# Tanh over two PSUM banks in the last group but one, and newly written instruction orders, in a fused linear-attention and tanh-shrink kernel

## The chip, the cores and the metric

The kernel runs on one core of one Trainium2 chip. The time is device microseconds (us) of one execution. Before the change three runs gave 104.94, 103.58 and 104.55 us, a median of 104.55. Engines are named as the profile names them: PE (TensorE matmuls), PEld (its weight loads), DVE (VectorE), ACT (ScalarE), POOL (GpSimd), SP (SyncE, which here only issues DMAs). PSUM, the memory that PE writes, has 8 banks here, each 512 float32 columns on 128 partitions.

## The reference

Batch 4, heads 4, sequence 1088, head size 32, sketch size 8, feed-forward width 2048.

```python
def phi(x):                        # 32 -> 64 features, a product of two sketches
    a = einsum('rd,bhsd->bhsr', S1, x)
    b = einsum('rd,bhsd->bhsr', S2, x)
    return einsum('bhsi,bhsj->bhsij', a, b).reshape(..., 64)
q_p, k_p = phi(q), phi(k)
kv  = einsum('bhsf,bhsd->bhfd', k_p, v);   z = sum(k_p, axis=2)
num = einsum('bhsf,bhfd->bhsd', q_p, kv)
den = einsum('bhsf,bhf->bhs', q_p, z)[..., None] + 1e-6
x   = (num / den) laid out as 4352 tokens x 128
h   = x @ w_in                     # 128 -> 2048
out = (h - tanh(h)) @ w_out        # 2048 -> 128
```

## The kernel before

The work has two halves. The **attention front** makes `xT` (128 features x 4352 tokens, bf16) in five chunks, called u=0 to u=4: batch 0 in two chunks, the other three batches in one each. The **layers** take the tokens in nine groups, g=0 to g=8: eight of 512 columns and a last one of 256. A group needs the chunks that hold its tokens: groups 0 and 1 need chunks 0 and 1, group 2 needs chunk 2, group 4 needs chunk 3, and groups 6, 7 and 8 need chunk 4.

In a group there are 16 blocks of 128 hidden units. For each, `h<n>` (L809) is one matmul of `w_in` by `xT` into a PSUM bank, `t<n>` (L813, or L818) is the tanh on ACT from that bank into the SBUF tile `tt`, and `o<n>` (L867, or L832 in the last group) is one matmul of `w_out` by the tanh that adds into PSUM bank 7. n counts through: h0 to h15 are group 0, h16 to h31 are group 1, and so on to h128 to h143, which are group 8. The part of the output that is linear, h times w_out, doesn't go through the hidden layer: `wp` multiplies the two weights once, split in a high and a low bf16 part (`whi`, `wlo`), and `lin<g>.whi` and `lin<g>.wlo` (L859; L832 for group 8) are two matmuls a group into the same bank 7. In all groups but group 0 they come first and clear the bank. After the last o of a group, `out<g>` (L872) on DVE transposes bank 7 into `osb`, which four or eight DMAs on SP store (`st<g>...`). So `lin` of the next group has to wait for `out` of the group before, since there is one accumulator, and all the o of the group stand behind their `lin`. Group 8 has its own accumulators, banks 0 and 1.

An h of a single tanh takes bank 4, 5 or 6 by n mod 3. A group in the list `PAIRS` puts two h side by side and has one tanh for both: before, this is group 8 alone, where two h of 256 columns share one bank.

The names in the front that matter below, with b the batch and u the chunk: `k<b>`, `q<b>`, `v<b>` are loads; `kT` a transpose on DVE (L511); `kp` a projection on PE (L522); `kab` its transpose on DVE (L528); `wk` products on DVE and POOL (L543); `sum` the matmuls of the key products with v (L591); `gram` and `fold` (L554, L578) the denominators; `qp` a projection on PE (L696); `qab`, `au`, `dn`, `rd`, `an`, `qm`, `qt` steps on DVE (`qm` half on POOL) that end in transposed query products; `num` (L741) the matmuls into banks 0 to 3; `x<u>` (L764) the copy to `xT`. `wi0` to `wi3` and `wo0`, `wo1` are loads of the two weights, `wic` and `woc` the casts to bf16 (`wic1` and both `woc` on POOL).

What stands where is not found by a scheduler at run time. `ORDERS` holds one list of names for each engine, and the instructions are emitted in that order; `SESSIONS` is a list of names that says in which order the users of a PSUM bank follow each other; `GATES` adds waits (a<b: a waits for b). `P.arranged` reads the three, and `sync` then places semaphore waits where one engine needs another's result. Each engine runs its list in order, so that a waiting instruction holds all that stand behind it. An entry such as `*12` in the list of PE is twelve matmuls on zeros ahead of the real work.

Of the kernel before, what the change touches and what calls it, by code (L numbers as in the profile page):

```python
# [971 lines left out]
```

## Time and profile before

| | |
|---|---|
| three runs | 104.94, 103.58, 104.55 us |
| the profiled execution | 103.87 us, of which the span of the profile is 102.1 us |
| busy: PE, ACT, DVE, PEld, POOL | 95.2, 79.2, 63.3, 44.0, 22.8 us |
| DMA | 11.74 MB, 115 GB/s over the span |
| matmuls h (L809) and o (L867) | 144 and 128, 45.8 and 39.5 us busy |
| tanh of 512 columns (L813) | 128, 66.8 us busy, 603 ns each |
| first and last tanh | start at 15.52 and 97.98 us |

Busy time of PE counts each matmul from its start to its modelled end, and the next one starts before that, so that the distance between two starts says more than the length of one. All times within the execution are counted from the start of the span.

### The profile page before, as it was taken

Reading aid. Unit: us, or ns where it says so; the run is one execution under the profiler, and the core shown is the slowest. Engines: PE = TensorE matmul, PEld = TensorE weight load, DVE = VectorE, ACT = ScalarE, POOL = GpSimd, SP = SyncE. Lnnn points to the kernel's source line nnn. Section 1 sums busy time; section 2 is a strip of 40 time slices with the busy share of each in tenths; the row PEclk is TensorE's granted clock in tenths of the full one; section 3 lists DMA queues with packets and bytes.
Section 4 is the critical chain, followed back from the end, with each engine's and each line's share of the span. In section 5 each row is a group of like instructions: output and inputs, shape, how many; then the busy total and the mean of one; then the engine's idle time right before and its main releaser. Section 6 shows DMA issues by size and latency. Waiting matters only on the chain.

```text
span 102.1 us, 2878 instructions
## 1 busy us (share of the span) xinstructions
PE 95.2 (93%) x1215; PEld 44.0 (43%) x1215; DVE 63.3 (62%) x109; ACT 79.2 (78%) x158; POOL 22.8 (22%) x36
## 2 busy tenths in 40 slices
PE   5978977989999999999999999999999999999980
PEld 2314632334736654334653334344334444435660
DVE  4589887999699998999968629595080020020210
ACT  4105428998889282599999999999999999998770
POOL 5306243085463160054080000700000000000000
PEclk9999999999999999999999999999999999999999
DMA  2899999997997059009700110035003204204143
GB/s 59 253 270 293 350 344 281 271 258 66 230 231 220 20 65 285 9 0 155 217 7 6 29 26 0 6 55 89 8 0 53 43 6 85 50 9 72 22 77 80
DMA packets 26012, 11.74 MB, mean 115 GB/s; under 512 B 19984, under 2 KB 24208, under 8 KB 26000
## 3 DMA queue, kind: packets, MB, share of 16 engines
q1 hardware_dynamic: 25712, 11.42, 49.4%
q8 instruction: 9, 0.15, 0.6%
q10 hardware_dynamic: 288, 0.15, 0.5%
q14 instruction: 3, 0.02, 0.1%
HBM read 8.81 MB, written 2.23 MB: 108 GB/s over the span
## 4 chain that ended last, share of the span: by engine, by line
PE 69%; DVE 12%; DMA 9%; SPq 5%; issue 1%
PE ps L809 26%; PE ps L867 25%; DMA kraw<-in_k_dram 9%; PE ps L741 5%; PE ps L859 4%; PE ps L591 2%; PE ps L696 2%; PE ps L832 2%; DVE qab L702 2%; DVE qp L719 2%; SPq L473 2%; DVE qpT L726 2%; DVE kT L511 1%; PE ps L522 1%; SPq L458 1%
## 5 line engine op out<-in xcount | busy, mean ns | idle before, releaser
L813 ACT ACTIVATE tt<-ps 128x512 bf16<-128x512 f32 x128 | 66.8, 603 | 6.1 <-PE ps L809 5.1
L809 PE MATMUL ps<-xT,w_in 128*128 128x512 bf16 (+1 forms) x144 | 45.8, 369 | 0.9 <-ACT tt L813 0.6
L867 PE MATMUL ps<-tt,w_out 128*128 128x512 bf16 x128 | 39.5, 379 | 0.1
L809 PEld LDWEIGHTS ps<-xT,w_in 128*128 128x128 bf16 x144 | 13.3, 98 | 20.9 <-ACT tt L813 9.0
L872 DVE STREAM_TRANSPOSE osb<-ps 128x512 f32<-128x512 f32 x8 | 5.7, 715 | 20.3 <-PE ps L867 20.3
L867 PEld LDWEIGHTS ps<-tt,w_out 128*128 128x128 bf16 x128 | 12.4, 98 | 13.4 <-issue 0.9
L719 POOL TENSOR_TENSOR qp<-an,qab 128x1152 f32<-128x1152 f32 (+1 forms) x4 | 7.8, 1953 | 21.6 <-DVE an L713 11.2
L543 POOL TENSOR_TENSOR wk<-kab 128x384 f32<-128x384 f32 (+2 forms) x8 | 9.0, 1126 | 13.7 <-DVE wk L543 13.2
L726 DVE STREAM_TRANSPOSE qpT<-qp 128x1152 f32<-128x1152 f32 (+1 forms) x8 | 9.8, 1229 | 1.1 <-POOL qp L719 1.0
L764 DVE CAST xT<-ps 128x576 bf16<-128x576 f32 (+2 forms) x7 | 4.4, 681 | 5.1 <-PE ps L741 5.1
L543 DVE TENSOR_TENSOR wk<-kab 128x768 f32<-128x768 f32 (+2 forms) x7 | 5.8, 842 | 0.9 <-PE ps L591 0.8
L511 DVE STREAM_TRANSPOSE kT<-kraw 128x512 f32<-128x512 f32 (+1 forms) x8 | 5.5, 718 | 1.2 <-DMA kraw<-in_k_dram 1.2
L702 DVE STREAM_TRANSPOSE qab<-ps 128x1152 f32<-128x1152 f32 (+1 forms) x4 | 5.0, 1239 | 1.9 <-PE ps L696 1.8
L741 PE MATMUL ps<-qpT,ndw 32*32 32x288 f32 (+3 forms) x256 | 5.7, 373 | 0.2 <-DVE qpT L726 0.2
L623 DVE STREAM_TRANSPOSE qT<-qraw 128x1088 f32<-128x1088 f32 (+2 forms) x5 | 5.3, 1070 | 0.0
L409 PE MATMUL ps<-wz 128*128 128x512 bf16 x12 | 4.2, 524 | 1.2 <-DVE wz L416 1.2
L719 DVE TENSOR_TENSOR qp<-an,qab 128x1152 f32<-128x1152 f32 (+1 forms) x4 | 5.1, 1276 | 0.1
L818 ACT ACTIVATE tt<-ps 128x512 bf16<-128x512 f32 x8 | 4.3, 598 | 0.8 <-PE ps L809 0.7
L591 PE MATMUL ps<-wk,vx 128*32 128x64 f32 x288 | 4.9, 220 | 0.1
L591 PEld LDWEIGHTS ps<-wk,vx 128*32 128x32 f32 x288 | 4.2, 110 | 0.9 <-issue 0.6
L741 PEld LDWEIGHTS ps<-qpT,ndw 32*32 32x32 f32 x256 | 2.5, 103 | 2.9 <-issue 1.2
L522 PE MATMUL ps<-kT,wkm 64*32 64x288 f32 x64 | 2.9, 415 | 0.7 <-DVE kT L511 0.7
(90 smaller groups left out, 73.7 us busy)
## 6 DMA issues: line engine op xcount, KB each, us to landing
kraw<-in_k_dram SPq DMA_DIRECT2D x3, 544.0 KB, 9.7
qraw<-in_q_dram SPq DMA_DIRECT2D x3, 544.0 KB, 4.7
out_dram<-osb SPq DMA_DIRECT2D x20, 64.0 KB, 1.9
vx<-in_v_dram SPq DMA_DIRECT2D x8, 144.0 KB, 4.3
vx<-in_v_dram SPq DMA_DIRECT2D x8, 128.0 KB, 4.2
w_in_f<-in_moe_w_in_dram SPq DMA_DIRECT2D x4, 256.0 KB, 9.4
w_out_f<-in_moe_w_out_dram SPq DMA_DIRECT2D x2, 512.0 KB, 10.0
kraw<-in_k_dram SPq DMA_DIRECT2D x1, 288.0 KB, 3.3
```

The source lines that it names most:

```text
L511: P.op(f"kT{b}.{cs[0]}", "vector", dve(hi - lo), lambda e, cs=cs, n=n, lo=lo, hi=hi: e.transpose(out=kT[i][:, 0:n, cs[0]:cs[1] + 1, :].rea ...
L543: P.op(f"wk{b}.{n0}", eng, (dve if eng == "vector" else pool)(64 * n), lambda e, n0=n0, n1=n1, n=n, a_=a_: e.tensor_tensor(out=wk[0][:, n0 ...
L591: ins = e.matmul(ps[32 * h:32 * h + 32, SB, 0:64], vx[i][:, h, t, :], wk[0][:, 4 * t + h, :], start=(t == 0), stop=(t == 8), tile_position ...
L623: P.op(f"qT{b}.{lo}", "vector", dve(32 * (hi - lo)), lambda e: e.transpose(out=dst, in_=src), r=[("qraw", i, c) for c in range(lo, hi)], w ...
L702: P.op(f"qab{u}", "vector", dve(32 * n), lambda e: e.transpose(out=qab[ui][:, 0:n, :].rearrange("p (h t) x -> p h t x", h=H), in_=ps[:, b0 ...
L719: P.op(f"qm{u}.{h0}", eng, (pool if eng == "gpsimd" else dve)(64 * (n1 - n0)), lambda e, n0=n0, n1=n1, b_=b_: e.tensor_tensor(out=qp[ui][: ...
L726: P.op(f"qt{u}.{h0}", "vector", dve(64 * (n1 - n0)), lambda e, n0=n0, n1=n1: e.transpose(out=qpT[ui][:, n0:n1, :, :].rearrange("p n y j -> ...
L741: ins = e.matmul(ps[32 * h:32 * h + 32, ct, 0:32 * own[ct]], ndw[i][32 * ct:32 * ct + 32, y, 32 * h:32 * h + 32], qpT[ui][32 * ct:32 * ct ...
L809: P.op(f"h{s}", "tensor", pe(n), lambda e, jb=jb, bk=bk, col=col: e.matmul(ps[:, bk, col:col + n], w_in[:, 128 * jb:128 * jb + 128], xT[:, ...
L813: P.op(f"t{s}", "scalar", act(n), lambda e, ts=ts, bk=bk: e.activation(out=tt[:, ts, 0:n], in_=ps[:, bk, 0:n], func=AF.Tanh, scale=-1.0), ...
L867: P.op(f"o{slot + jb}", "tensor", pe(n), lambda e, jb=jb, ts=ts: e.matmul(acc[:, 0:n], w_out[:, jb, :], tt[:, ts, 0:n], start=late and jb ...
L872: P.op(f"out{g}", "vector", dve(n), lambda e: e.transpose(out=osb[u][:, 0:n], in_=acc[:, 0:n]), r=ka, w=[("osb", u)], prio=when)
```

## The change

Three things change together. First, group 7 joins `PAIRS`: its 16 tanh of 512 columns become 8 of 1024, each over two neighbouring banks. The two banks of a pair were written as 2, 3 and 0, 1 in turn for such a group; now they are 2, 3 and 4, 5. Second, all five lists of `ORDERS`, `SESSIONS` and four of the `GATES` are written anew. Third, two settings are added that do nothing at the values given: `ENDS` is empty, so the last store is the one of before, and `K1CUTS` has one piece, so the load of `k1` is the one of before.

```diff
-PAIRS = (8,)
+PAIRS = (7, 8)
+ENDS = ()
+K1CUTS = ((0, 1088),)
...
-*12 kp0 qB0 gram0 qA0 zs eps1 fold0 eps0 sum0.0 den0 den1 kwt num0.1 num0.0 turn0 h0 qp1 h2 h1 h3 o0 h4 o1 h5 h6 kp1
+*13 kp0 qB0 gram0 qA0 fold0 eps1 zs eps0 sum0.0 den0 den1 kwt num0.0 num0.1 turn0 h0 h1 qp1 h2 o0 h3 h4 o1 o2 h5 h6
...
-k0.1 s1 k0.0 q0.0 v0.0 v0.1 v0.2 v0.3 q0.1 wi0 wo0 k1.0 wi1 wi2 wi3 v1.1 v1.2 k2.0 wo1 v1.3 v1.0 q1.0 wT v2.0 v2.2
+k0.1 s1 k0.0 q0.0 v0.0 v0.1 v0.2 v0.3 wi0 q0.1 k1.0 wo0 wi1 wi2 wi3 v1.3 v1.0 k2.0 v1.1 v1.2 wo1 q1.0 wT v2.3 v2.0
...
-identb<wk2.0 wic1<wk0.0 woc0<wk0.0 woc1<wk1.24 wk0.22<wk0.0 wk0.29<wk0.0 qm1.2<qm1.0 wk1.12<qm1.0 wk1.30<qm1.0
-qm2.2<qm2.0 wk2.12<wk2.24 wk2.30<wk2.0 qm3.2<qm3.0 wk3.12<wk3.24 wk3.30<wk3.24 qm4.2<an4
+identb<qm2.0 wic1<wk0.0 woc0<wk0.0 woc1<wk1.0 wk0.22<wk0.0 wk0.29<wk0.0 qm1.2<qm1.0 wk1.12<qm1.0 wk1.30<qm1.0
+qm2.2<qm2.0 wk2.12<wk2.24 wk2.30<wk2.0 qm3.2<qm3.0 wk3.12<qm2.0 wk3.30<qm2.0 qm4.2<qm4.0
...
             if g in PAIRS:
                 x, bk, col = s // 2, 4 + s // 2 % 3, 256 * (jb % 2)
                 if n > 256:
-                    bk, col = (2, 0)[s // 2 % 2] + jb % 2, 0
+                    bk, col = (2, 4)[s // 2 % 2] + jb % 2, 0
                 kh = bank(f"h{s - jb % 2}", bk)
...
-    load_k(1, 0, S, L + 11)
+    for x, (lo, hi) in enumerate(K1CUTS):
+        load_k(1, lo, hi, L + 11 + 0.1 * x, x)
```

Line numbers of the changed kernel are 2 higher from the settings on, and 8 or 9 higher behind the store of the last group: h is L811, the tanh of a pair L820, o L875, `lin` L867.

What the new lists move is seen best in the built programs, at three places: the start of the layers (SP and PE), the last groups (PE and ACT), and the loads of `v3` (SP). At the start, the loads on SP from the second piece of `q0` on, before the change:

```order
L464 DMA qraw<-in_q_dram 128x576
L479 DMA w_in_f<-in_moe_w_in_dram 128x512
L483 DMA w_out_f<-in_moe_w_out_dram 128x8x128
L458 DMA kraw<-in_k_dram 128x1088
L479 DMA w_in_f<-in_moe_w_in_dram 128x512 x3
```

The same place after the change:

```order
L481 DMA w_in_f<-in_moe_w_in_dram 128x512
L466 DMA qraw<-in_q_dram 128x576
L460 DMA kraw<-in_k_dram 128x1088
L485 DMA w_out_f<-in_moe_w_out_dram 128x8x128
L481 DMA w_in_f<-in_moe_w_in_dram 128x512 x3
```

The first quarter of `w_in` now goes ahead of the rest of `q0`, and `k1` goes ahead of the first half of `w_out`.

On PE the first matmuls of the layers, from `turn0` (ident by kvz) to the sixth or seventh h (xT by w_in), with `qp1` (qT by wq) and the first o (tt by w_out) between, before the change:

```order
L610 MATMUL ps<-ident,kvz 128x128 x2
L809 MATMUL ps<-xT,w_in 128x512
L696 MATMUL ps<-qT,wq 32x160 x16
L809 MATMUL ps<-xT,w_in 128x512 x3
L867 MATMUL ps<-tt,w_out 128x512
L809 MATMUL ps<-xT,w_in 128x512
L867 MATMUL ps<-tt,w_out 128x512
L809 MATMUL ps<-xT,w_in 128x512 x2
```

The same place after the change:

```order
L612 MATMUL ps<-ident,kvz 128x128 x2
L811 MATMUL ps<-xT,w_in 128x512 x2
L698 MATMUL ps<-qT,wq 32x160 x16
L811 MATMUL ps<-xT,w_in 128x512
L875 MATMUL ps<-tt,w_out 128x512
L811 MATMUL ps<-xT,w_in 128x512 x2
L875 MATMUL ps<-tt,w_out 128x512 x2
L811 MATMUL ps<-xT,w_in 128x512 x2
```

The first o stood behind four h and stands behind three; h3 and h4, which were ahead of and behind it, are both behind it now.

In the last groups, on PE, the passage from group 5 to group 6, from the last five or so o (tt by w_out) of group 5 to `lin6` (xT by whi and by wlo), before the change:

```order
L867 MATMUL ps<-tt,w_out 128x512 x3
L809 MATMUL ps<-xT,w_in 128x512
L867 MATMUL ps<-tt,w_out 128x512
L809 MATMUL ps<-xT,w_in 128x512
L867 MATMUL ps<-tt,w_out 128x512
L832 MATMUL ps<-wlo,xT 128x128 x2
L809 MATMUL ps<-xT,w_in 128x512 x3
L859 MATMUL ps<-xT,whi 128x512
L859 MATMUL ps<-xT,wlo 128x512
```

The same place after the change:

```order
L811 MATMUL ps<-xT,w_in 128x512 x2
L875 MATMUL ps<-tt,w_out 128x512 x5
L811 MATMUL ps<-xT,w_in 128x512 x5
L867 MATMUL ps<-xT,whi 128x512
L867 MATMUL ps<-xT,wlo 128x512
```

Between the last o of group 5 and `lin6` there were three h (and the small `lin8.wlo`, which moves to near the end); now there are five h, two of which are h116 and h117 of group 7.

On ACT, the tanh from `ndw3` (a copy of the last batch's sums) on, before the change:

```order
L616 COPY ndw<-ps 128x256
L813 ACTIVATE tt<-ps 128x512 x73
L818 ACTIVATE tt<-ps 128x2x256 x8
L846 COPY osr<-ps 128x128
```

The same place after the change:

```order
L618 COPY ndw<-ps 128x256
L815 ACTIVATE tt<-ps 128x512 x47
L820 ACTIVATE tt<-ps 128x1024
L815 ACTIVATE tt<-ps 128x512 x9
L820 ACTIVATE tt<-ps 128x1024
L815 ACTIVATE tt<-ps 128x512
L820 ACTIVATE tt<-ps 128x1024 x2
L820 ACTIVATE tt<-ps 128x2x256
L820 ACTIVATE tt<-ps 128x1024 x4
L820 ACTIVATE tt<-ps 128x2x256 x7
L848 COPY osr<-ps 128x128
```

The tanh of groups 6, 7 and 8 are mixed: the first pair of group 7 (t112) stands among the single tanh of group 6, ahead of its last nine but one, and the first pair of group 8 (t130) among those of group 7.

At the third place, on SP, from the load of `k3` or its neighbours to the first stores, with the loads of `v3` (vx) between, before the change:

```order
L458 DMA kraw<-in_k_dram 128x1088
L879 DMA out_dram<-osb 32x16x32
L464 DMA qraw<-in_q_dram 128x1088
L473 DMA vx<-in_v_dram 32x4x288
L879 DMA out_dram<-osb 32x16x32 x3
L473 DMA vx<-in_v_dram 32x4x256
```

The same place after the change:

```order
L466 DMA qraw<-in_q_dram 128x1088
L460 DMA kraw<-in_k_dram 128x1088
L466 DMA qraw<-in_q_dram 128x1088
L887 DMA out_dram<-osb 32x16x32
L475 DMA vx<-in_v_dram 32x4x288
L887 DMA out_dram<-osb 32x16x32
L475 DMA vx<-in_v_dram 32x4x256
L475 DMA vx<-in_v_dram 32x4x288
```

`q2` and `q3` now go ahead of all stores. Of the four loads of `v3`, two stood behind the first store and three do now. That first store was `st0.0.0`, of group 0; now it is `st1.0.2`, of group 1, which waits for `out1`. Before, the first store of group 1 stood three stores later, with one load of `v3` behind it.

88 lines of the change are left out of this document (47 added, 41 removed).

## The prediction

> **What bounds the kernel.** I began with the page: busy times, the chain that ended last, and the costliest groups.
>
> ```profile
> span 102.1 us, 2878 instructions
> PE 95.2 (93%) x1215; PEld 44.0 (43%) x1215; DVE 63.3 (62%) x109; ACT 79.2 (78%) x158; POOL 22.8 (22%) x36
> PE 69%; DVE 12%; DMA 9%; SPq 5%; issue 1%
> L813 ACT ACTIVATE tt<-ps 128x512 bf16<-128x512 f32 x128 | 66.8, 603 | 6.1 <-PE ps L809 5.1
> ```
>
> The chain is on PE for 69% of the span, and ACT, whose work the change makes less, waits for PE (5.1 us at L813) and holds little of the chain. So the question is not what the wider tanh saves, but how long PE stands. I cut the time into stretches, of which two late ones are these (columns: PE, PEld, DVE, ACT, POOL busy, each with its instructions, then granted clock, DMA share, GB/s).
>
> ```profile
> 82.00:90.00 8.00, 8.00 (x39) 3.49 (x38) 0.72 (x1) 7.68 (x16) 0.00 (x0) 1.00 0.26 45
> 90.00:98.00 8.00, 7.94 (x59) 4.64 (x58) 1.44 (x2) 6.77 (x14) 0.00 (x0) 1.00 0.20 33
> ```
>
> PE is all but full in both. But its ends are modelled and overlap the next start, so short stands don't show in a busy share. They show in the distance of starts, in the timeline of PE:
>
> ```profile
> 36.93 1.67 PE L867 MATMUL ps<-tt,w_out 128*128 128x512 bf16 x7
> ...
> 65.25 1.03 PE L809 MATMUL ps<-xT,w_in 128*128 128x512 bf16 x3
> 66.30 0.39 PE L859 MATMUL ps<-xT,whi 128*128 128x512 bf16 x1
> ...
> 75.88 0.38 PE L809 MATMUL ps<-xT,w_in 128*128 128x512 bf16 x1
> 76.28 0.39 PE L859 MATMUL ps<-xT,whi 128*128 128x512 bf16 x1
> ...
> 82.88 0.97 PE L809 MATMUL ps<-xT,w_in 128*128 128x512 bf16 x3
> 83.82 0.39 PE L859 MATMUL ps<-xT,whi 128*128 128x512 bf16 x1
> ...
> 89.87 1.02 PE L809 MATMUL ps<-xT,w_in 128*128 128x512 bf16 x3
> 90.92 0.39 PE L859 MATMUL ps<-xT,whi 128*128 128x512 bf16 x1
> ```
>
> Seven o take 1.67 us, the last of them some 0.38, so one follows the other after (1.67 - 0.38) / 6 = 0.215 us. Three h should thus take 0.65 us until the next start. Ahead of lin4 they took 1.05 (a stand of 0.40), ahead of lin6 0.94 (0.29), ahead of lin7 1.05 (0.40), and the one h ahead of lin5 took 0.40 (0.18). Together **1.27 us of standing at the four passages between groups**. What ends them is the accumulator:
>
> ```profile
> 65.03 0.38 PE L867 MATMUL ps<-tt,w_out 128*128 128x512 bf16 x1
> 65.52 0.72 DVE L872 STREAM_TRANSPOSE osb<-ps 128x512 f32<-128x512 f32 x1 [1.25 <-PE ps L867]
> ```
>
> From the start of the last o (65.03) to lin4 (66.30) lie 1.27 us: the o, the transpose of 0.72 us, two hand-overs. In that time only h are free to run, and only as far as their banks are.
>
> **The change part by part.** *Wide tanh.* What one of 1024 columns takes, no row shows. Nearest rows of ACT:
>
> ```profile
> 50.72 0.37 ACT L604 COPY kvz<-ps 128x256 f32<-128x256 f32 x1
> 96.53 2.07 ACT L818 ACTIVATE tt<-ps 128x512 bf16<-128x512 f32 x4 [0.21 <-PE ps L809]
> ```
>
> One alone takes 0.60 us (603 ns above); four follow each other after (2.07 - 0.60) / 3 = 0.49. From 256 to 512 columns a row grows by 0.60 - 0.37 = 0.23 us, so 1024 columns hold ACT for between 2 x 0.46 = 0.92 us (growth alone) and two whole rows, 1.20; I take 0.95, near the growth, since the rows overlap. Against 0.98 for two this saves 8 x 0.03 = 0.2 us of ACT, or costs 1.8 at the other end. ACT has 1.2 us free between 90 and 98 (6.77 of 8.00), so I count the saving at nothing, and at the bad end 1.8 - 1.2 = 0.6 us.
>
> *Banks.* This is what I expect the gain from. Group 7 writes banks 2 to 5 in turn, so that h112, h113, h116 and h117 go into banks 2 and 3, which were empty there. At lin6 five h instead of three stand between the last o of group 5 and lin6, 5 x 0.215 = 1.08 us, and the o itself 0.22: 1.30 against 1.27, so nothing is left to stand for: -0.29. At lin7 the order has h130, h121, h131, h120, h122, h123 there (four whole, two half, 1.08): -0.40. At lin5 it has h91, h96, h112, h95, h113, h94 and the small lin8.whi: 1.40 against a lin5 that the three copies of x4 and out4 hold as before; -0.18, of which I leave 0.10 for h94, whose bank waits for t91: -0.08. At lin4 three h stand as before, one of them with a bank freed earlier: -0.10. Sum **-0.87**. At the very end, h140 waits for t134's bank and o142 for the last tanh; I take +0.10.
>
> *Start.* Here the loads are reordered. POOL, DVE and SP:
>
> ```profile
> 5.85 0.44 SPq L483 DMA_DIRECT2D w_out_f<-in_moe_w_out_dram  x1
> 6.34 0.77 SPq L458 DMA_DIRECT2D kraw<-in_k_dram  x1
> 7.15 2.83 SPq L479 DMA_DIRECT2D w_in_f<-in_moe_w_in_dram  x3
> ...
> 14.00 1.04 POOL L773 CAST w_out<-w_out_f 128x1024 bf16<-128x1024 f32 x1 [3.10 <-DMA w_out_f<-in_moe_w_out_dram]
> 16.06 1.37 DVE L511 STREAM_TRANSPOSE kT<-kraw 128x576 f32<-128x576 f32 x2 [1.02 <-DMA kraw<-in_k_dram]
> 16.83 0.61 POOL L770 CAST w_in<-w_in_f 128x512 bf16<-128x512 f32 x1 [1.43 <-DMA w_in_f<-in_moe_w_in_dram]
> ```
>
> Issued as wo0, k1, wi1, they were used as they landed, at 14.00, 16.06 and 16.83. With k1 ahead, k1 lands about when wo0 did and wo0 when k1 did, 16.06, the bytes up to there being the same. kT1 then starts behind x0 without its wait of 1.02 us, and the chain of DVE for chunk 1 is 1.0 us ahead. But the cast of w_out, 1.04 us, ends at 17.10 and not at 15.04, and o0 needs it. wic1 is behind it on POOL: 17.10 + 0.61 = 17.71, against 17.44.
>
> ```profile
> 16.64 0.38 PE L867 MATMUL ps<-tt,w_out 128*128 128x512 bf16 x1
> 17.64 0.38 PE L809 MATMUL ps<-xT,w_in 128*128 128x512 bf16 x1 [0.62 <-ACT tt L813]
> ...
> 20.02 0.63 ACT L770 CAST w_in<-w_in_f 128x512 bf16<-128x512 f32 x1
> ...
> 22.75 1.14 PE L741 MATMUL ps<-qpT,ndw 32*32 32x160 f32 x64 [0.18 <-DVE qpT L726]
> ```
>
> Before, PE stood 17.64 - 16.64 - 0.22 = 0.78 us ahead of h4 for wic1. Now it stands at o0 until 17.15, h3 follows at 17.37 and h4 at 17.77: 0.13 later with the same work done. From there ACT sets the pace, since h7 to h12 each need a bank: t3 17.75, t4 18.24, t5 18.86, the cast wic2 (0.5 of pace by the row at 20.02), t6 to t8, the cast wic3, t9 to 22.4, and h12, which needs t9's bank and wic3, at 22.45. num1 follows at 22.78, against 22.75, with one o fewer done (o7, 0.22): **+0.25**. The gain of DVE buys nothing, since qt1, which released num1 at 22.75 before, is done by some 22.0 (1.0 earlier, less a wait for kp1), and num1 waits for its place on PE.
>
> The other exchange on SP, wi0 ahead of the rest of q0:
>
> ```profile
> 11.01 0.77 DVE L623 STREAM_TRANSPOSE qT<-qraw 128x576 f32<-128x576 f32 x1
> ...
> 12.47 0.88 DVE L666 STREAM_TRANSPOSE osb<-ps 128x256 f32<-128x256 f32 x2 [0.28 <-PE ps L652]
> ...
> 11.29 0.62 ACT L770 CAST w_in<-w_in_f 128x512 bf16<-128x512 f32 x1 [0.80 <-DMA w_in_f<-in_moe_w_in_dram]
> ```
>
> The cast on ACT started as wi0 landed, 11.29; q0 now lands about then, and its transpose, at 11.01, waits 0.28 us. DVE idles 0.28 us at 12.47, which hides it: nothing, or what a later landing adds beyond that, up to 0.3 us. I count nothing.
>
> Does the 0.25 reach the end? Behind num1 come sum1, then DVE:
>
> ```profile
> 26.06 1.21 PE L591 MATMUL ps<-wk,vx 128*32 128x64 f32 x72
> 27.41 0.56 DVE L543 TENSOR_TENSOR wk<-kab 128x384 f32<-128x384 f32 x1 [0.85 <-PE ps L591]
> ...
> 37.51 1.38 DVE L726 STREAM_TRANSPOSE qpT<-qp 128x1152 f32<-128x1152 f32 x1 [0.22 <-POOL qp L719]
> 38.96 1.57 PE L741 MATMUL ps<-qpT,ndw 32*32 32x288 f32 x64
> ```
>
> DVE waits for sum1, then works without a gap through qp2's chain to 37.51 + 1.38 = 38.89, and num2 starts at 38.96 where PE has just ended its h and o. Both paths are tight, and the same instructions stand between in the new lists (out0 and gm2 only change places). So it goes through, and group 2 starts 0.25 later.
>
> **Sum**: +0.25 - 0.87 + 0.10 = -0.52 us on the profiled execution, 103.87 to 103.35. That execution lies 0.68 below the median of the three runs, 104.55; on that median I say **104.0 us**.
>
> A page of the Trainium skill bears on the start: "DMA: Bandwidth & Descriptors", in "Two DMAs through the same engine are not ordered", says that descriptors of one queue start in order but are pipelined, and that nothing orders transfers across the 16 engines. The three landings above come in issue order, so here the trace goes by the order of issue. Were the transfers free of it, wo0 might land as early as before, the wait at o0 would go, the start term would be near +0.13, and the time 103.9 in place of 104.0.
>
> **Rivals.**
>
> *wo0 lands late, and the kernel is slower.* Landing of the w_out loads, in us after their issue (least, median, most):
>
> ```profile
> DMA to landing us min/median/max: 8.1/10.0/11.9
> ```
>
> Issued behind k1's 0.77 us, wo0 goes out at 6.66 and lands at 14.8, 16.7 or 18.6. Each us behind 16.06 holds o0 and with it every matmul behind, one for one. At 16.6 the whole forecast gain is gone; at the far end it is +2.5 - 0.5 = +2.0: 106.5 us. I price it at half the far end, 1.2 us on the forecast: 105.2. For it speaks that PE has nothing else to do there; against it that bytes ahead of wo0 don't grow.
>
> *v3 lands late.* Three loads of v3 stand behind st1.0.2, which waits for out1. The row of the load that stood there before, sum3, and the landings of all v:
>
> ```profile
> 45.51 0.49 SPq L473 DMA_DIRECT2D vx<-in_v_dram  x1
> ...
> 49.44 1.21 PE L591 MATMUL ps<-wk,vx 128*32 128x64 f32 x72
> ...
> DMA to landing us min/median/max: 2.9/4.2/9.2
> ```
>
> The last goes out three issues later, about 46.9, and lands at 49.8, 51.1 or 56.1. sum3 stands five h and o later than before, at 49.44 + 1.08 + 0.25 = 50.8. So it decides from a landing of 3.9 us on, near the median; the most costs PE 5.3 us. These landings are mostly of the crowded start; I price it at 1.2 us too: 105.2.
>
> *The front pays after all*: the landing of wo0 costs nothing, and DVE's 1.0 us at the start is kept to num2, since PE is held less than I think: -0.87 + 0.10 - 1.0 = -1.77, 102.8.
>
> *Nothing changes*: the passages keep their 1.27 us, since the freed banks wait for ACT anyway, and the start costs 0.25: 104.8.
>
> **Chances.** Forecast 0.50, wo0 late 0.17, v3 late 0.08, front pays 0.12, nothing 0.13. The forecast's own range is 103.2 to 104.8. Three runs here spread by 1.36 us, so about 2% is what tells a change from none: 102.46 and 106.64. Faster than that: the front rival with a spread of 0.4 us below it, and little of the forecast, 0.13. Slower: the far ends of both late loads and of the tanh, 0.14. The range leaves about a tenth out on each side: 102.4 (the front pays, and a little more) to 106.0 (late loads beyond their price, or the tanh's 0.6 us on top of one).
>
> **What would show it.** In the profile after: starts of h to lin6 and lin7 spaced by 0.22 without a stand; an ACT row of 1024 columns near 1.03 us; the cast of w_out on POOL starting near 16.1 and kT1 near 15.1 without a wait; num1 at 22.8; num2 near 39.2. I am wrong if sum3 waits for a DMA, if DVE reaches num2 after PE, if the pairs of h stand for two banks at once, or if o0 comes behind 17.7.

## The result and the profile after

Twenty runs of each kernel: **103.86 us after** (103.34 to 104.56) against **104.41 before** (103.58 to 104.94), a ratio of **0.9957, interval 0.9939 to 0.9975**. By the bound of 2% that is no change; with twenty runs a small gain of 0.3 to 0.6 us is seen all the same. Ratios, here and below, are taken over the single executions and not from the medians, and leave out executions more than 1.5% above the shortest of their kernel: four of the twelve of run 11, its profiled one among them, and one or two in four other sets. The profiled execution took 103.72 us, with a span of 101.7.

The page of the changed kernel: span, busy time of each engine, shares of the chain that ended last, and the two groups of tanh (busy, mean ns of one, idle time ahead of them):

```profile
span 101.7 us, 2860 instructions
PE 93.0 (91%) x1201; PEld 43.9 (43%) x1216; DVE 62.8 (62%) x109; ACT 78.1 (77%) x150; POOL 22.8 (22%) x36
PE 75%; ACT 13%; DMA 5%; issue 2%; SPq 2%; DVE 1%
L815 ACT ACTIVATE tt<-ps 128x512 bf16<-128x512 f32 x112 | 58.4, 609 | 6.4 <-PE ps L811 5.2
L820 ACT ACTIVATE tt<-ps 128x1024 bf16<-128x1024 f32 (+1 forms) x16 | 12.3, 810 | 0.5 <-PE ps L811 0.3
```

ACT now holds 13% of the chain; before, the row of its engines didn't name it. Some records of matmuls are missing here (1201 on PE, 1216 weight loads on PEld), h0's too, so PE's 93.0 is not less work. The two late stretches, columns as before:

```profile
82.00:90.00 8.00, 7.95 (x39) 3.63 (x38) 1.32 (x2) 7.64 (x14) 0.00 (x0) 1.00 0.25 43
90.00:98.00 8.00, 7.95 (x63) 4.97 (x63) 0.83 (x2) 7.84 (x12) 0.00 (x0) 1.00 0.29 49
```

PE's share says as little as before. ACT's in the second stretch went from 6.77 to 7.84 of 8.00 us: the slack of 1.2 us there is used up. The passages between groups, in the timeline of PE (start, length, count):

```profile
65.33 0.38 PE L875 MATMUL ps<-tt,w_out 128*128 128x512 bf16 x1
65.59 0.98 PE L811 MATMUL ps<-xT,w_in 128*128 128x512 bf16 x3
66.59 0.39 PE L867 MATMUL ps<-xT,whi 128*128 128x512 bf16 x1
...
75.31 1.03 PE L811 MATMUL ps<-xT,w_in 128*128 128x512 bf16 x4
76.27 0.29 PE L834 MATMUL ps<-whi,xT 128*128 128x128 bf16 x2
76.39 0.59 PE L811 MATMUL ps<-xT,w_in 128*128 128x512 bf16 x2
76.82 0.38 PE L867 MATMUL ps<-xT,whi 128*128 128x512 bf16 x1
...
82.44 1.24 PE L811 MATMUL ps<-xT,w_in 128*128 128x512 bf16 x5
83.52 0.38 PE L867 MATMUL ps<-xT,whi 128*128 128x512 bf16 x1
...
89.13 1.25 PE L811 MATMUL ps<-xT,w_in 128*128 128x256 bf16 x6
90.21 0.38 PE L867 MATMUL ps<-xT,whi 128*128 128x512 bf16 x1
```

I count 0.215 us for an o or a whole h, and half of it for a narrow h. From the start of the last o of group 3 to lin4 it takes 1.26 us as before, and 0.40 of it is standing as before; only 0.04 of the stand moved ahead of the first h. Ahead of lin5 the first four h took 0.96 (a stand of 0.10) and the last two 0.43 (none). Before, there were three h. The first two of them took 0.53, a stand of 0.10 that the prediction didn't count:

```profile
75.23 0.59 PE L809 MATMUL ps<-xT,w_in 128*128 128x512 bf16 x2
75.76 0.28 PE L832 MATMUL ps<-whi,xT 128*128 128x128 bf16 x2
```

The third took 0.40 (a stand of 0.18), so lin5's passage stood 0.28 before and stands 0.10 now. Five h took 1.08 ahead of lin6, and four whole and two narrow ones 1.08 ahead of lin7, and nothing stood: the stands of 0.29 and 0.40 there are gone.

The start, in the timelines of POOL, DVE and PE:

```profile
14.05 1.04 POOL L775 CAST w_out<-w_out_f 128x1024 bf16<-128x1024 f32 x1 [2.71 <-DMA w_out_f<-in_moe_w_out_dram]
15.22 0.61 POOL L772 CAST w_in<-w_in_f 128x512 bf16<-128x512 f32 x1
...
15.87 1.36 DVE L513 STREAM_TRANSPOSE kT<-kraw 128x576 f32<-128x576 f32 x2
...
16.24 0.38 PE L811 MATMUL ps<-xT,w_in 128*128 128x512 bf16 x1 [0.46 <-DVE xT L676]
17.03 0.39 PE L811 MATMUL ps<-xT,w_in 128*128 128x512 bf16 x1
17.26 0.38 PE L875 MATMUL ps<-tt,w_out 128*128 128x512 bf16 x1
17.48 0.59 PE L811 MATMUL ps<-xT,w_in 128*128 128x512 bf16 x2
...
22.88 1.14 PE L743 MATMUL ps<-qpT,ndw 32*32 32x160 f32 x64
```

The first row of h is h1; h0 ran 0.22 ahead of it, at 16.02. The cast of w_out starts at 14.05 and not at 16.06, o0 stands for nothing, and num1 comes 6.86 us after h0; before the change it was 22.75 - 15.09 = 7.66. But h0 itself is 0.93 later than in the execution before.

sum3 waits for a load of v3 (issues on SP, and weight loads of PE):

```profile
46.68 0.97 SPq L475 DMA_DIRECT2D vx<-in_v_dram  x2
...
51.03 1.05 PEld L593 LDWEIGHTS ps<-wk,vx 128*32 128x32 f32 x72 [0.39 <-DMA vx<-in_v_dram]
```

### The profile page after: what moved, and what is told of

Read it like the earlier page. It is cut to its first block, busy times and chain, and to the rows that moved or that the text cites. A ratio compares the mean times of both kernels' runs of the same rounds, so it can differ in the third digit from the quotient of the medians.

```text
span 101.7 us, 2860 instructions
## 1 busy us (share of the span) xinstructions
PE 93.0 (91%) x1201; PEld 43.9 (43%) x1216; DVE 62.8 (62%) x109; ACT 78.1 (77%) x150; POOL 22.8 (22%) x36
## 4 chain that ended last, share of the span: by engine, by line
PE 75%; ACT 13%; DMA 5%; issue 2%; SPq 2%; DVE 1%
PE ps L875 24%; PE ps L811 24%; ACT tt L815 12%; PE ps L743 5%; PE ps L593 5%; DMA qraw<-in_q_dram 5%; PE ps L867 3%; PE ps L834 2%; PE ps L636 2%; PE ps L654 2%; PE ps L612 2%; PE ps L556 1%; PE ps L580 1%; ACT w_in L772 1%; SPq L460 1%
## 5 line engine op out<-in xcount | busy, mean ns | idle before, releaser
L815 ACT ACTIVATE tt<-ps 128x512 bf16<-128x512 f32 x112 | 58.4, 609 | 6.4 <-PE ps L811 5.2
L811 PE MATMUL ps<-xT,w_in 128*128 128x512 bf16 (+1 forms) x134 | 42.6, 368 | 1.6 <-ACT tt L815 0.9
L875 PE MATMUL ps<-tt,w_out 128*128 128x512 bf16 x124 | 38.0, 379 | 0.7 <-issue 0.3
L811 PEld LDWEIGHTS ps<-xT,w_in 128*128 128x128 bf16 x144 | 13.5, 98 | 21.3 <-ACT tt L815 9.4
L875 PEld LDWEIGHTS ps<-tt,w_out 128*128 128x128 bf16 x128 | 12.4, 98 | 13.0 <-issue 0.7
L820 ACT ACTIVATE tt<-ps 128x1024 bf16<-128x1024 f32 (+1 forms) x16 | 12.3, 810 | 0.5 <-PE ps L811 0.3
L545 DVE TENSOR_TENSOR wk<-kab 128x384 f32<-128x384 f32 (+2 forms) x7 | 5.7, 824 | 1.0 <-PE ps L593 0.9
L411 PE MATMUL ps<-wz 128*128 128x512 bf16 x13 | 4.7, 538 | 1.2 <-DVE wz L418 1.2
L606 ACT COPY kvz<-ps 128x256 f32<-128x256 f32 x4 | 1.5, 377 | 3.6 <-PE ps L593 2.0
```

The source lines that it names most:

```text
L545: P.op(f"wk{b}.{n0}", eng, (dve if eng == "vector" else pool)(64 * n), lambda e, n0=n0, n1=n1, n=n, a_=a_: e.tensor_tensor(out=wk[0][:, n0 ...
L811: P.op(f"h{s}", "tensor", pe(n), lambda e, jb=jb, bk=bk, col=col: e.matmul(ps[:, bk, col:col + n], w_in[:, 128 * jb:128 * jb + 128], xT[:, ...
L815: P.op(f"t{s}", "scalar", act(n), lambda e, ts=ts, bk=bk: e.activation(out=tt[:, ts, 0:n], in_=ps[:, bk, 0:n], func=AF.Tanh, scale=-1.0), ...
L820: P.op(f"t{s - 1}", "scalar", act(2 * n), lambda e, ts=ts, src=src: e.activation(out=tt[:, ts - 1:ts + 1, 0:n], in_=src, func=AF.Tanh, sca ...
L875: P.op(f"o{slot + jb}", "tensor", pe(n), lambda e, jb=jb, ts=ts: e.matmul(acc[:, 0:n], w_out[:, jb, :], tt[:, ts, 0:n], start=late and jb ...
```

## The experiments

Times are medians on the same chip as the runs of the kernel before that stand with them: 104.37 for the first four kernels, 104.31 for the next four, 104.37 for the last four.

### 1. The changed kernel again

No edit.

> The changed kernel once more, to have it on the same chip as the next two and to see its start a second time. In its first profile k0 and q0 landed at 6.04 and 7.13 us, against 5.21 and 6.02 in the profile of before, though the issues up to there are the same; h0 began 1.15 us later, and num1 only 0.13 later. If that is a matter of the execution, k0 lands near 5.2 here, h0 begins near 15.1 and num1 near 22.0; if the change brings it (w_in's first quarter ahead of the rest of q0), k0 lands near 6.0 again. Time: 0.9957 of before within 0.003 either way.

Measured: 103.76 us, 0.9944 (0.9910 to 0.9977). `k0.0` landed at 5.72 us and h0 started at 15.68, between the two cases named. sum3's weights waited longer:

```profile
51.16 1.05 PEld L593 LDWEIGHTS ps<-wk,vx 128*32 128x32 f32 x72 [0.84 <-DMA vx<-in_v_dram]
```

The last h ahead of it started at 50.40, and the time from there to sum3 is 0.46 us more than in the profile after (50.72 to 51.03). So the late v3 costs PE between nothing and 0.46 us in these two profiles.

### 2. Each tanh of 1024 columns as two of 512, one behind the other

The semaphores stay as they are: one signal for the pair.

```diff
-                P.op(f"t{s - 1}", "scalar", act(2 * n), lambda e, ts=ts, src=src: e.activation(
-                    out=tt[:, ts - 1:ts + 1, 0:n], in_=src, func=AF.Tanh, scale=-1.0),
+                def halves(e, ts=ts, src=src):
+                    if n <= 256:
+                        return e.activation(out=tt[:, ts - 1:ts + 1, 0:n], in_=src, func=AF.Tanh, scale=-1.0)
+                    for y in range(2):
+                        ins = e.activation(out=tt[:, ts - 1 + y, 0:n], in_=src[:, y, :], func=AF.Tanh, scale=-1.0)
+                    return ins
+
+                P.op(f"t{s - 1}", "scalar", act(2 * n), halves,
```

> The changed kernel with each tanh of 1024 columns made of two of 512, one behind the other, with the same wait ahead of both and the same release behind both; orders and banks unchanged. In the profile after, a tanh of 1024 holds ACT for 0.91 us and two of 512 for some 0.97, and ACT works without a gap over 0.3 us from 80 us to the end. Theory that the width is worth nothing, since PE sets the end (as predicted): the same time as the changed kernel within 0.2 us. Rival, that ACT sets the end of the changed kernel: 8 x 0.06 = 0.5 us longer, so the time of before.

Measured: 104.06 us, 0.9948 (0.9908 to 0.9988), not to be told from the changed kernel. The timelines of ACT, of the changed kernel first and of the split one behind it (L820 and L824 are the same pairs):

```profile
80.54 1.02 ACT L820 ACTIVATE tt<-ps 128x1024 bf16<-128x1024 f32 x1
81.44 4.61 ACT L815 ACTIVATE tt<-ps 128x512 bf16<-128x512 f32 x9
86.31 1.02 ACT L820 ACTIVATE tt<-ps 128x1024 bf16<-128x1024 f32 x1 [0.25 <-PE ps L811]
87.23 0.59 ACT L815 ACTIVATE tt<-ps 128x512 bf16<-128x512 f32 x1
87.70 10.49 ACT L820 ACTIVATE tt<-ps 128x1024 bf16<-128x1024 f32 x14
```

```profile
80.55 1.08 ACT L824 ACTIVATE tt<-ps 128x512 bf16<-128x512 f32 x2
81.50 4.56 ACT L815 ACTIVATE tt<-ps 128x512 bf16<-128x512 f32 x9
86.31 1.08 ACT L824 ACTIVATE tt<-ps 128x512 bf16<-128x512 f32 x2 [0.25 <-PE ps L811]
87.29 0.60 ACT L815 ACTIVATE tt<-ps 128x512 bf16<-128x512 f32 x1
```

A wide tanh holds ACT for 81.44 - 80.54 = 0.90 and 87.23 - 86.31 = 0.92 us until the next can start; two halves hold it for 0.95 and 0.98. In the run of nine singles one follows the other after (4.61 - 0.60) / 8 = 0.50. So the width saves 0.05 to 0.09 us a pair. From sum3 to the last o the split kernel took 47.54 us and the changed one 47.34: 0.2 us, which the profile shows and the times can't. Part of it is a stand that comes back ahead of lin7, in the split kernel on PE:

```profile
89.14 1.37 PE L811 MATMUL ps<-xT,w_in 128*128 128x256 bf16 x6
90.35 0.38 PE L873 MATMUL ps<-xT,whi 128*128 128x512 bf16 x1
```

The six h took 1.21 us there, for 1.08 in the changed kernel.

### 3. Two of the five h back from ahead of lin6 to behind it

```diff
-h116 h117 h106 h104 lin6.whi lin6.wlo h111 o96 h109 o97 o98 h107 o99 h114 o100 h115 o101 h110 o102 o103 o104 o105 o106
+h106 h104 lin6.whi lin6.wlo h116 h117 h111 o96 h109 o97 o98 h107 o99 h114 o100 h115 o101 h110 o102 o103 o104 o105 o106
```

> The changed kernel with h116 and h117 moved on PE from ahead of lin6 to right behind it; nothing else. If the h of group 7 in the banks 2 and 3 are what fills the passage, PE stands some 0.4 us ahead of lin6 again (0.29 in the profile of before, none after). Theory that PE sets the end: 0.3 to 0.4 us longer than the changed kernel. Rival that ACT sets the end there: the stand returns, and the time stays within 0.15 us.

Measured: 104.26 us, 1.0003 (0.9968 to 1.0038). PE at the passage:

```profile
82.51 1.04 PE L811 MATMUL ps<-xT,w_in 128*128 128x512 bf16 x3
83.55 0.39 PE L867 MATMUL ps<-xT,whi 128*128 128x512 bf16 x1
```

Three h took 1.04 us, a stand of 0.40, and from sum3 to the last o it took 47.75 us for 47.34. So two h moved behind the next four entries of PE's list are worth the whole stand to the end, and nothing behind makes it good: PE's list sets the end. In the times the two h bring back 0.4 to 0.5 us, about the whole gain, and in the profile 0.41.

### 4. The kernel before again

No edit.

> The kernel before once more, for a second profile of its start: if the landing of k0 (5.21 us in the first profile) varies from execution to execution, it may be some tenths of a us or up to 0.9 us later here, with h0 shifted by as much; if it is fixed, 5.2 again.

Measured: 104.25 us in one execution, span 102.5. `k0.0` landed at 5.83 us for 5.21, and h0 started at 15.75 for 15.09, so its landing isn't fixed. The other loads landed otherwise too, the order of the program being the same (timelines of POOL and PE):

```profile
12.89 1.04 POOL L773 CAST w_out<-w_out_f 128x1024 bf16<-128x1024 f32 x1 [1.33 <-DMA w_out_f<-in_moe_w_out_dram]
14.93 0.61 POOL L770 CAST w_in<-w_in_f 128x512 bf16<-128x512 f32 x1 [0.64 <-DMA w_in_f<-in_moe_w_in_dram]
...
17.30 0.38 PE L867 MATMUL ps<-tt,w_out 128*128 128x512 bf16 x1
18.29 0.38 PE L809 MATMUL ps<-xT,w_in 128*128 128x512 bf16 x1 [0.62 <-ACT tt L813]
```

w_out was there at 12.89 for 14.00, and `wic1` started at 14.93 for 16.83. The prediction took these landings from one execution as fixed. And h4 still stood 18.29 - 17.30 - 0.22 = 0.77 us, though wic1 had ended at 15.54. So that stand was never a wait for wic1. The row names the cause, `<-ACT tt`: h4 takes bank 5 behind h1 (both are 1 by n mod 3), and needs t1, which stood third on ACT, behind t2.

### 5. The last three loads of v3 ahead of all stores

```diff
-v2.2 v2.1 v3.3 q2.0 k3.0 q3.0 st1.0.2 v3.1 st0.0.0 v3.2 v3.0 st0.0.3 st0.0.2 st0.0.1 st2.2.1 st1.0.0 st2.0.2 st1.0.1
+v2.2 v2.1 v3.3 q2.0 k3.0 q3.0 v3.1 v3.2 v3.0 st1.0.2 st0.0.0 st0.0.3 st0.0.2 st0.0.1 st2.2.1 st1.0.0 st2.0.2 st1.0.1
```

> The changed kernel with v3.1, v3.2 and v3.0 moved on SP from behind the stores st1.0.2 and st0.0.0 to right behind q3.0, ahead of all stores; nothing else. In the profiles of the changed kernel so far sum3 began at 51.03 to 51.16 us and waited for v3 each time, 0.4 to 0.8 us on the weight load, while num1 began anywhere from 22.55 to 22.96. If the late v3 takes back what the front gains, sum3 follows num1 by 28.15 us or less and begins before 51.0, and the time is 0.2 to 0.5 us below the changed kernel (0.992 of before). Rival: PE makes up for the wait elsewhere, since its backlog of o is the same: the wait goes, the time stays within 0.1 us.

Measured: 103.62 us, 0.9946 (0.9920 to 0.9971), span 101.2.

```profile
50.51 1.05 PEld L593 LDWEIGHTS ps<-wk,vx 128*32 128x32 f32 x72 [0.39 <-issue]
```

No wait for a DMA, and num1 to sum3 takes 28.15 us as in the profile after, where v3 was just in time; in run 1 it took 28.61. In the times the difference to the changed kernel, 0.1 to 0.2 us, is not beyond the intervals.

### 6. The old front with the new last groups

All lists as before the change up to num4 (on DVE, POOL and SP, and the gates, to the end); the new PE, ACT and sessions from num4 on, and both pairs.

```diff
-*13 kp0 qB0 gram0 qA0 fold0 eps1 zs eps0 sum0.0 den0 den1 kwt num0.0 num0.1 turn0 h0 h1 qp1 h2 o0 h3 h4 o1 o2 h5 h6
+*12 kp0 qB0 gram0 qA0 zs eps1 fold0 eps0 sum0.0 den0 den1 kwt num0.1 num0.0 turn0 h0 qp1 h2 h1 h3 o0 h4 o1 h5 h6 kp1
...
-k0.1 s1 k0.0 q0.0 v0.0 v0.1 v0.2 v0.3 wi0 q0.1 k1.0 wo0 wi1 wi2 wi3 v1.3 v1.0 k2.0 v1.1 v1.2 wo1 q1.0 wT v2.3 v2.0
+k0.1 s1 k0.0 q0.0 v0.0 v0.1 v0.2 v0.3 q0.1 wi0 wo0 k1.0 wi1 wi2 wi3 v1.1 v1.2 k2.0 wo1 v1.3 v1.0 q1.0 wT v2.0 v2.2
```

> Half of the change: all lists of before up to num4 and on DVE, POOL and SP throughout; from num4 on the new orders of PE, ACT and the banks, with group 7 in pairs on banks 2 to 5. Theory that the last passages are the whole gain and the front is worth nothing or a little less: no stand ahead of lin6 and lin7, 0.7 to 0.9 us below before (0.992). If the front of the change gains as well, this one is slower than the changed kernel by that.

Measured: 103.67 us, 0.9951 (0.9927 to 0.9976): the gain of the changed kernel with the old front. From lin5 to the last o it takes 21.55 us like the changed kernel, 22.50 before; from h0 to num1 7.40, like the kernel before (7.66 and 7.41). One h fewer stands in that stretch with the new lists; the rest is the stands at lin6 and lin7, which are gone. The one ahead of h4 is back. From h0 to the last o it takes 82.88 us, 0.52 more than run 5. Yet the times of the two, 103.67 and 103.62 on the same chip, agree: 0.25 us of the difference lies outside the span (see the end of this section).

### 7. The new front with the old last groups

The opposite: old PE, ACT and sessions from num4 on, `PAIRS = (8,)`.

```diff
-PAIRS = (7, 8)
+PAIRS = (8,)
...
-h85 o74 h87 o75 o76 h86 num4.0 h90 h88 h89 num4.1 h93 h92 o77 o78 o79 h91 h96 h112 h95 lin8.whi h113 h94 lin5.whi
+h85 o74 h87 o75 o76 h86 num4.0 h88 h89 h90 h91 num4.1 h93 h92 h94 o77 o78 o79 h96 h95 lin8.whi h97 lin5.whi h99
```

> The other half: the new lists of the change up to num4 and on DVE, POOL and SP throughout; from num4 on the orders of before, group 7 single on banks 4 to 6. By the prediction the front costs 0.25 us and the stands at lin5, lin6 and lin7 are back: 0.1 to 0.3 us above before (1.002). If the front gains net of the wait for v3: at or below before (0.996 to 1.000).

Measured: 105.26 us, 1.0110 (1.0079 to 1.0142). The tail takes its old time (22.49 us from lin5 to the last o). But the seam is not clean: one h behind num4 and the small lin8.whi stood 0.42 and 0.27 us (no such stand behind num4 in the kernel before, and 0.10 ahead of lin8.whi), and sum3 stood 0.37 for v3. From h0 to the last o it took 84.30 us against 83.69 and 83.44; less 1.06 of these stands it would be 83.24. So the front alone is worth 0.2 to 0.45 us within the span by this profile, as an argument from stands; as a time it wasn't measured cleanly.

### 8. As run 5, with the first h and tanh in the old order

```diff
-*13 kp0 qB0 gram0 qA0 fold0 eps1 zs eps0 sum0.0 den0 den1 kwt num0.0 num0.1 turn0 h0 h1 qp1 h2 o0 h3 h4 o1 o2 h5 h6
+*13 kp0 qB0 gram0 qA0 fold0 eps1 zs eps0 sum0.0 den0 den1 kwt num0.0 num0.1 turn0 h0 qp1 h2 h1 h3 o0 h4 o1 o2 h5 h6
...
-s2 wab0 wab1 kap0 bq.1 bq.0 zw kvz0 kvw wic0 ndw0 t0 t1 t2 t3 t4 t5 wic2 t6 t7 t8 wic3 t9 t10 t11 t12 x1.0 x1.2 t13
+s2 wab0 wab1 kap0 bq.1 bq.0 zw kvz0 kvw wic0 ndw0 t0 t2 t1 t3 t4 t5 wic2 t6 t7 t8 wic3 t9 t10 t11 t12 x1.0 x1.2 t13
```

> e5 with the first h in the order of before on PE and ACT (h0 qp1 h2 h1 h3 o0 h4, and t0 t2 t1 t3 t4); the loads stay in the new order. From h0 to num1 the profiles of before take 7.4 to 7.7 us, those of the changed kernel 6.6 to 6.9. If the order of the first h does that (h4 waits for the bank of t1, which comes third on ACT before), the stand of 0.8 us ahead of h4 is back and h0 to num1 takes 7.3 us or more. If the loads do it, it stays at 6.9, with no stand ahead of h4.

Measured: 104.49 us, 1.0028 (0.9999 to 1.0058), where run 5 on the same chip had 0.9946. On PE, o0 and h4:

```profile
17.89 0.38 PE L875 MATMUL ps<-tt,w_out 128*128 128x512 bf16 x1
18.89 0.38 PE L811 MATMUL ps<-xT,w_in 128*128 128x512 bf16 x1 [0.62 <-ACT tt L815]
```

The stand of 18.89 - 17.89 - 0.22 = 0.78 us is back, with k1 ahead of wo0 and wic1 long done. h0 to num1 takes 7.47 us for 6.86, and all of it goes through: h0 to the last o 82.97 for 82.36. That is the gain of the front within the span, and it is one of order: h1 and t1 ahead of `qp1` and t2.

### 9 to 12. The head of SP's list, and two casts on POOL

All four have v3 early, as run 5; run 12 is that kernel again. Run 9 puts the rest of q0 ahead of wi0 as before the change, run 10 wo0 ahead of k1 as well, and run 11 is run 9 with the casts `wic2` and `wic3` on POOL.

```diff
-k0.1 s1 k0.0 q0.0 v0.0 v0.1 v0.2 v0.3 wi0 q0.1 k1.0 wo0 wi1 wi2 wi3 v1.3 v1.0 k2.0 v1.1 v1.2 wo1 q1.0 wT v2.3 v2.0
+k0.1 s1 k0.0 q0.0 v0.0 v0.1 v0.2 v0.3 q0.1 wi0 k1.0 wo0 wi1 wi2 wi3 v1.3 v1.0 k2.0 v1.1 v1.2 wo1 q1.0 wT v2.3 v2.0
...
-k0.1 s1 k0.0 q0.0 v0.0 v0.1 v0.2 v0.3 wi0 q0.1 k1.0 wo0 wi1 wi2 wi3 v1.3 v1.0 k2.0 v1.1 v1.2 wo1 q1.0 wT v2.3 v2.0
+k0.1 s1 k0.0 q0.0 v0.0 v0.1 v0.2 v0.3 q0.1 wi0 wo0 k1.0 wi1 wi2 wi3 v1.3 v1.0 k2.0 v1.1 v1.2 wo1 q1.0 wT v2.3 v2.0
...
-WIC = ('scalar', 'gpsimd', 'scalar', 'scalar')
+WIC = ('scalar', 'gpsimd', 'gpsimd', 'gpsimd')
```

> The changed kernel with v3 ahead of the stores (as in the run with v3 early) and, in addition, the rest of q0 issued ahead of wi0 again, as before the change. Theory: in the changed kernel the first piece of k0 lands late because wi0, issued earlier, shares the DMA engines with it; h0 then comes late by the same amount. The first piece of k0 lands at 5.2 to 5.5 us (5.5 to 6.5 in the seven profiles with wi0 first, 5.2 to 5.8 in the three with q0 first), h0 starts near 15.5 instead of 15.9 on average, and the time is 0.3 to 0.4 us below that of the run with v3 early on the same chip. Rival: the landing of k0 varies by itself from run to run: h0 anywhere from 15.1 to 16.4, and a time within 0.15 us of the run with v3 early.

> As the run before, and wo0 ahead of k1 as well: the whole head of SP's list up to wi1 is that of before the change, while PE and ACT keep the new order. Theory: what the front gained (h0 to num1 6.86 us instead of 7.41 to 7.66) comes from the order of the first h and their tanh, not from k1 being issued ahead of wo0: h0 to num1 stays at 6.8 to 6.9, and the time is within 0.15 us of the run with q0 first. Rival: the lead of k1 is what the front gained: kT1 on DVE waits 0.6 to 1.0 us for k1, num1 comes 0.5 us later (h0 to num1 7.4), and the time is 0.5 us longer.

> The run with q0 first, and the casts of the third and fourth quarter of w_in on POOL instead of ACT. Of the 6.86 us from h0 to num1 some 1.05 us are stands ahead of h for banks, since ACT does 9 tanh and two casts of about 0.5 us of its pace there. Theory: without the casts PE is free earlier, but num1 then waits for the last transpose of DVE's chain, which ends at 22.1 where num1 began at 22.36: h0 to num1 6.5 to 6.65, and the time 0.2 to 0.35 us below the run with q0 first; it would be the fastest of all, near 103.0. Rival A: the casts on POOL slow DVE or come too late for h9: no gain or up to 0.3 us longer. Rival B: the front is not on the path: num1 comes earlier, the start of sum3 counted from h0 stays, and the time is the same.

> The kernel with v3 ahead of the stores again, unchanged, as the one that the other three of this call are compared with. All theories: 103.4 to 103.9 us, no wait of sum3 for a DMA, h0 to the last o 82.3 to 82.9 us. The theory of wi0: the first piece of k0 lands later here than in the run with q0 first. The rival: the landings overlap.

Measured: run 9 103.75 us, 0.9961 (0.9934 to 0.9988); run 10 103.68, 0.9928 (0.9900 to 0.9955); run 11 104.97, 1.0029 (0.9991 to 1.0067), its runs spread from 103.73 to 107.13; run 12 103.68, 0.9934 (0.9906 to 0.9963).

**Run 9.** The theory on wi0 falls. In the timeline of DVE the transpose of the piece `k0.0` starts as it lands, here at 6.41, later than in any profile with wi0 first but one; in run 12, with wi0 first, it starts at 5.64:

```profile
6.41 0.78 DVE L513 STREAM_TRANSPOSE kT<-kraw 128x576 f32<-128x576 f32 x1 [1.19 <-DMA kraw<-in_k_dram]
```

**Run 10.** Timelines of DVE and POOL:

```profile
12.91 1.04 POOL L775 CAST w_out<-w_out_f 128x1024 bf16<-128x1024 f32 x1 [1.61 <-DMA w_out_f<-in_moe_w_out_dram]
...
15.82 1.36 DVE L513 STREAM_TRANSPOSE kT<-kraw 128x576 f32<-128x576 f32 x2
```

w_out's load lands first again, 1.4 us sooner than in run 9 (14.32 there, 12.85 here), and k1 at 14.22 for 12.58. DVE comes to k1's transpose at 15.82 and waits for neither. num1 comes 6.86 us after h0. So with these landings the exchange of k1 and wo0 is worth nothing either way.

**Run 11.** Timelines of POOL, DVE and PE:

```profile
18.92 0.61 POOL L772 CAST w_in<-w_in_f 128x512 bf16<-128x512 f32 x1 [1.31 <-DMA w_in_f<-in_moe_w_in_dram]
...
19.14 0.57 DVE L715 TENSOR_TENSOR an<-qab,rd 128x160 f32<-128x160 f32 x1
...
22.87 1.14 PE L743 MATMUL ps<-qpT,ndw 32*32 32x160 f32 x64 [0.94 <-DVE qpT L728]
...
28.44 1.09 PE L593 MATMUL ps<-wk,vx 128*32 128x64 f32 x60 [1.62 <-issue]
```

Without the two casts ACT no longer holds h7 to h12, but num1 then waits 0.94 us for the last transpose of DVE's chain, and comes 6.94 us after h0, not sooner. In run 9, which has the casts on ACT, that transpose ends only 0.21 us ahead of num1 (23.07 and 23.28). So DVE's chain is right behind ACT as the bound. The step `an` took 0.57 us in this profile, while the cast ran on POOL, and 0.33 in run 9; that the cast lengthened it is likely but not tested. The stand of 1.62 us within sum1 is in this profile alone, of an execution that took 105.52 us; what PE waited for there the profile doesn't show. Why this kernel isn't only without a gain, but longer than run 9, stays unexplained.

### What the profiles give together

The profiled execution's own time, less the start of h0 (from h1 less 0.22 where h0's record is missing):

| kernel | h0 | time | time from h0 on | stand of sum3 for v3 |
|---|---|---|---|---|
| before; again | 15.09; 15.75 | 103.87; 104.25 | 88.78; 88.50 | none |
| after; run 1 | 16.02; 15.68 | 103.72; 103.89 | 87.70; 88.21 | 0; 0.46 |
| v3 early: runs 5, 12, 9, 10 | 15.50, 15.56, 16.42, 15.97 | 103.24, 103.30, 104.15, 103.67 | 87.74, 87.74, 87.73, 87.70 | none |
| run 2, two halves | 15.87 | 103.89 | 88.02 | 0.15 |
| run 3, two h back | 16.09 | 104.21 | 88.12 | 0 |
| run 6, old front | 15.70 | 103.67 | 87.97 | none |
| run 8, old first h | 16.43 | 104.74 | 88.31 | none |

Runs 7 and 11 are left out for the other stands that they have. The four profiles with v3 early have the same time from h0 on within 0.04 us, and times that differ by 0.9. So what differs between these executions is when `k0.0` lands and h0 can start, 9.9 to 10.5 us behind it in every profile. From h0 on the change saves 88.50 to 88.78 less 87.70, that is **0.8 to 1.1 us**, of which up to 0.46 goes in an execution where v3 is late.

The span doesn't hold all of the time, and what lies outside it isn't the same in the two kernels. The time of an execution less its span, which is listed to 0.1 us, is 1.73 to 1.85 us in all listed executions of the kernel before and of run 6, with medians of 1.77 to 1.79. In the changed kernel it is 1.98 to 2.08, median 2.03, and in all other runs but run 11 it is 1.98 to 2.10. So the change costs **0.25 us that no profile shows**, and within the span, from h0 to its end, it saves 1.1 to 1.3 us. Since run 6 doesn't have the cost and run 7 does, it comes with the new lists up to num4, those of DVE, POOL and SP, or the changed gates (five by the diff, not four), and not with the pairs. By runs 8 and 10 it is not the order of the first h nor the head of SP's list. What it is stays open.

## Why the prediction was right in its size and wrong in two steps

The forecast was 104.0 us, 103.35 for the profiled execution; measured were 103.86 and 103.72. The size came out near by luck, because errors of opposite sign stood in the sum.

**Passages, forecast -0.87: right in its sum and its mechanism.** Measured nothing at lin4, -0.18 at lin5, -0.29 at lin6, -0.40 at lin7: -0.87. The two parts that were wrong, -0.10 forecast at lin4 and -0.08 at lin5, cancel. Run 3 shows that it is the number of h ahead of lin6 that does it and that the stand reaches the end; run 6 has the gain without the new front, run 7 loses it. The rival that nothing changes is out.

**Tail, forecast +0.10: nothing.** From h143 to the last o it takes 1.46 us for 1.23, because 26 small matmuls stand behind h143 where 20 did. Counted as stands it is 0.08 us for 0.09.

**Width, forecast nothing: mis-sized by 0.2 us.** I took 0.95 us for which a wide tanh holds ACT, and 1.03 for the row; it is 0.90 to 0.92, and 1.02. The saving was to be hidden by 1.2 us of free ACT between 90 and 98. That cover was the time PE stood. With the stands gone ACT has 0.16 us free there, and in run 2 the narrow tanh bring back a stand of 0.13 us ahead of lin7 and push the last o back by 0.2 us. The Trainium skill ("ScalarE: Activation LUTs", "What ACT_TABLE_LOAD costs") states 186 ns and 0.833 ns a column for one ACTIVATE with immediate scale and bias, and that ACTIVATEs back to back overlap by about 93 ns. An estimate by this is 613 ns for 512 columns and 1039 for 1024, near the 609 of the row of singles and the 1.02 us here. By it a merge would save the 93 ns; the runs show 50 to 90.

**Start, forecast +0.25: the step that failed.** "k1 lands about when wo0 did and wo0 when k1 did, 16.06" took three landings of one execution for those of the kernel. In the changed kernel k1 landed at 12.2 and wo0 behind it at 14.0; in the kernel before, run again, wo0 landed at 12.8 and k1 behind it at 14.2. In all ten profiles with wo0 behind k1 it landed at 13.7 to 14.7, not at 16.06. So o0 had no wait, and the rival of the late wo0 didn't happen; that "bytes ahead of wo0 don't grow" was wrong all the same, since those of k1 now stand ahead of it. Run 9 and run 10 have these two landing in the order of issue both ways. The Trainium skill ("DMA: Bandwidth & Descriptors", "Two DMAs through the same engine are not ordered") states that nothing orders DMAs across the 16 engines. Other loads agree (`v1.1`, issued behind `k2`, landed at 20.31 and `k2` at 20.74 in run 9), but the landings of wo0 and k1 show no overtaking.

The second half of that step was misread: "PE stood 0.78 us ahead of h4 for wic1". The quoted row itself had `<-ACT tt`, and runs 4 and 8 show that it was t1, third on ACT. The new order sets h1 and t1 first, so that this stand goes: h0 to num1 takes 6.86 us, and with the one o that moved behind num1 (0.22) 7.08, against 7.41 to 7.66. That is -0.3 to -0.6 where I had +0.25. What the step says of DVE holds: the lead of k1 buys nothing (run 10). That ACT sets the pace to num1 holds too, though with DVE close behind (runs 9 and 11). The forecast of num1 at 22.8 was met at 22.88 for the wrong reasons: h0 came 0.9 later, and the way from it was 0.8 shorter.

**v3, a rival: true in its mechanism, small in its price.** sum3 waits for it in both profiles of the changed kernel, as "the last goes out three issues later" says. It decides near the time forecast (landing at 50.96 against sum3 at 50.8), but in all five profiles with these stores ahead (the changed kernel, its run 1, and runs 2, 3 and 7) that load landed 3.7 to 4.2 us after the start of its issue, near the median of 4.2 and not the most, 9.2, and the price was 0 to 0.46 us, not 1.2.

**Outside the span, not in the sum: +0.25.** The forecast took a gain within the span for one of the time. The new lists add 0.25 us outside it, as the paragraph behind the table shows, and the sum had no term for it.

**The front pays after all, a rival: true within the span, not in the time, and not by its mechanism.** From h0 to the last o the new front gains 0.52 us (run 5 against run 6), from the order of h1 and t1 and not from DVE's lead. But run 6, with the old front, took 103.67 us, and run 5 103.62: the time outside the span and the start take the gain back.

**Together.** From the profile before to the one after, h0 to the last o: -0.87 - 0.58 = -1.45 by the terms, -1.33 in the profile; from run 4 to the one after -0.87 - 0.33 = -1.20 and -1.08. The 0.12 us between terms and profile are not assigned. The times show -0.55, and -0.6 to -0.7 with v3 early. Of what is missing, 0.25 us lies outside the span, and the rest at the start: the medians less the time from h0 on give an h0 at 15.9 to 16.0 us with v3 early, and at 15.6 to 15.9 in the kernel before. `k0.0` landed at 5.2 to 5.8 us in the three profiles with the old lists and at 5.5 to 6.5 in the eleven with the new ones. The place of wi0 is not the cause (runs 9 and 10). Whether another part of the new lists is, or chance, stays open.

The versions with v3 early ran at 103.62 and 103.68, and are the shortest measured beside run 10's 103.68; by the intervals none is told from the changed kernel.

## What to carry to other kernels

Where an accumulator is shared between stages, count the work that may run between its last use and its next one: each such passage stands for transpose time less that work, and a few matmuls whose banks are free there are worth their full length, if their engine sets the end. A slack on another engine that is measured while the first one stands is not a cover once it doesn't. Read who released a wait from the row itself, and take landings of loads from more than one execution. And before a gain within the span is counted as one of the time, compare the time less the span in both kernels.
